# An attention and feed-forward kernel on one core: the steps of all five engines in one written list, in a new order, with PSUM as one tile of eight banks

## The chip, the cores and the metric

The kernel runs on one core of a Trainium2 chip. The core has five engines with an instruction queue each, which meet only through semaphores: TensorE (PE) for matmuls, ScalarE (ACT), VectorE (DVE), GpSimd (POOL), and SyncE (SP), which only starts DMAs. ACT and POOL can start DMAs too. Operands lie in SBUF; matmuls write to PSUM, which has eight banks of 512 f32 values per partition. The metric is the device time of one execution, in microseconds (us); lower is better.

## What is computed

Eight batches of attention with eight heads of width 64 over 576 positions, a causal window of 128 and a linear bias; then a feed-forward layer on its output, with a gated activation.

```python
B, H, S, D = q.shape                       # 8, 8, 576, 64
scores = (q @ k^T) / sqrt(D)
mask = (rel >= 0) & (rel < 128)            # rel = query position - key position
scores = where(mask, scores - slopes[h] * |rel|, -1e9)
attn = softmax(scores)
x = (attn @ v).transpose(0, 2, 1, 3).reshape(4608, 512)
h = x @ w_in                               # 512 -> 2048
g = h * (1.0 / (1.0 + exp(-beta * h)))
out = g @ w_out                            # 2048 -> 512, f32
```

Inputs and outputs are f32; the kernel multiplies in bf16 and accumulates in f32.

## The kernel before

**Attention.** q, k and v are loaded in f32 into staging tiles (`fst`, 14 buffers) and cast to bf16. For batches 0 and 1, full rows are handled by pairs of heads p = 0..3: q and k are cast into `bst` and transposed on PE (`TP`), and the result is copied to `QK`, for q by ACT and for k by DVE. For batches 2 to 7, and only there, blocks of 128 rows (sb = 0..4, the last of 64) are cast and then transposed by a DMA from SP (`DT`). The rows 512 to 575 of batches 0 and 1 have their own small steps (`TT`, `SCT`, `PV`, `X`).
Scores of K=64 go to two neighbouring banks of PSUM (`SP_` with the visits A and B for batches 0 and 1, `SC` for the others). ACT takes their exponential into `pt`, and DVE multiplies by a table of the bias and the mask (`factor`), unless a matmul has put the bias in beforehand ("biased"). Then `PVP` or `PVB` multiplies by v, with a column of ones for the sum; DVE divides (`norm`); and the result is transposed to `XT`, on PE (`XP`, `X`) for batches 0 to 3, by DMAs from SP for 4 to 7.

**Feed-forward.** The 4608 rows are cut into nine groups g of 512. Block `H(g, j)`, j = 0..15, is four matmuls 128x512 into one bank (`hps`, `hpo`, `SX`); ACT takes the tanh of half of beta*h (L564), and DVE forms (tanh + 1) * h into `gT` (L565). Output block (g, i), i = 0..3, is sixteen matmuls 128x512 in four parts `O(g, i, n)` (L588); then an eviction with the factor 0.5 into `osb` (L598, on ACT), and a store (L606). The last output block, (8, 3), is in two halves of 256 columns, in one bank; its second half is evicted by DVE (L596).

**What sets the order.** The first part, up to four H matmuls of j = 0 and 1, is written out by hand for all five engines, under `manual_schedule`. From there PE, SP and POOL follow the order in which the program's text issues steps, while ACT and DVE are ordered by the framework's scheduler. The text mixes steps by rules: `blocks(2)` with batch 2's loads, `jobs(b)` for later batches' loads, casts and transposes, `att` for attention steps with weights, and `spread` to deal them out between the H and O parts. PSUM comes from pools (`psum_c`, `psum_h`, `psum_t`, `psum_x`, later `psum_o`, `psum_s`), which decide the bank of each tile; a pool that is closed makes room for another.
All loads of q and k, and the first batches' v, are started by SP (L207, L218), all casts of loaded data are done by POOL (L228 to L243), which also starts the loads of the weights, W1 and W2 in four pieces each (L257, L261), and those of later v's (L250). Stores are started by POOL (g < 3), ACT and SP. Two gates hold steps back: the first DMA transpose of batch 2 waits for the last piece of W2, and `falls_late`, which fills a table, for the tanh of (1, 4).
A step in this text holds the matmuls and what ACT and DVE do with them. Idle matmuls on zeros (`idle`, `calm`) keep PE's clock up: 16 in all.

Of the kernel before, what the change touches and what calls it, by code (L numbers as in the profile page):

```python
# [15 lines left out]
P = 128  # L16


@with_exitstack
def kernel(  # L20
# [10 lines left out]
    nc = tc.nc  # L31
# [52 lines left out]
    psum_c = ctx.enter_context(tc.tile_pool(name="psum_c", bufs=1, space=bass.MemoryType.PSUM))  # L84
    psum_h = ctx.enter_context(tc.tile_pool(name="psum_h", bufs=2, space=bass.MemoryType.PSUM))
    trans = ExitStack()
    psum_t = trans.enter_context(tc.tile_pool(side="right", name="psum_t", bufs=2, space=bass.MemoryType.PSUM))
    SS = psum_c.tile([P, 2, 512], F32, name="SS")
    psum_c.seal()
    opening = ExitStack()  # L90
    psum_x = opening.enter_context(tc.tile_pool(name="psum_x", bufs=1, space=bass.MemoryType.PSUM))
    SX = psum_x.tile([P, 2, 512], F32, name="SX")
    late, gates = {"tick": 0}, {}
    spans = [SS]

    def span():

        spans.append(spans.pop(0))
        return spans[-1]

    def obank(name, tag=None):
        if tag is None:
            late["n"] = late.get("n", 0) + 1
            tag = "ops" if late["n"] % 2 else "h3"
        return late["o"].tile([P, DM], F32, name=name, tag=tag)[:]

    def after(ins, other):
        tc.add_manual_dep(
            ins.ins, other.ins.name,
            mybir.DependencyInfo(mybir.DependencyClass.Sync, mybir.DependencyReason.DATA),  # L110
            reason="gate",
        )

    def idle(n):
        for _ in range(n):
            nc.tensor.matmul(
                SS[:, 0, :], lhsT=zeros[:, 0:P], rhs=zeros[:], start=True, stop=True,
                skip_group_check=True)  # L120

    def constants():
# [4 lines left out]
        idle(8)  # L127
# [35 lines left out]
    def falls_late(i):  # L163
        to, a, w = ((0, 0, P), (128, 0, 64), (192, 0, P), (320, 1, 64), (384, 1, P))[i]
        after(nc.vector.tensor_copy(
            out=falls[:, :, to : to + w], in_=fall[:, :, a, 0:w]), gates[1, 4])

    def factor(pt, m, p):

        if m:  # L170
            nc.vector.tensor_tensor(  # L171
                out=pt[:], in0=pt[:], in1=falls[:, 2 * p : 2 * p + 2], op=ALU.mult)
            return
# [16 lines left out]
    def betas():  # L190
        bps = psum_t.tile([P, NFF], F32, name="bps", tag="t")
        nc.tensor.transpose(out=bps[:], in_=bflat[:], identity=identf[:])
        nc.vector.tensor_scalar_mul(beta_h[:], bps[:], 0.5)
# [7 lines left out]
    def get(what, b, sb):  # L201

        rows = ROWS[sb]
        src = {"q": q, "k": k, "v": v}[what]
        f = fst_pool.tile([P, H, D], F32, name="fst", tag="fst")
        fs[what, b, sb] = f
        return nc.sync.dma_start(  # L207
            out=f[0:rows],
            in_=src[b, :, P * sb : P * sb + rows, :].rearrange("h p d -> p h d"),
        )  # L210

    def get_pair(b, p):

        r = []
        for what, src in (("k", k), ("q", q)):
            f = fst_pool.tile([P, 2, 4, D], F32, name="fst", tag="fst")
            fs[what, b, "p", p] = f
            r.append(nc.sync.dma_start(  # L218
                out=f[:].rearrange("r h c d -> r h (c d)"),
                in_=src[b, 2 * p : 2 * p + 2, 0:FULL, :].rearrange("h (r c) d -> r h (c d)", c=4),  # L220
            ))
        return r[0]

    def cast_qk(b, sb):
        rows = ROWS[sb]
        t = bst_pool.tile([P, 2, H, D], BF16, name="bst", tag="bst")
        staged[b, sb] = t
        nc.gpsimd.tensor_copy(out=t[0:rows, 0], in_=fs.pop(("q", b, sb))[0:rows])  # L228
        return nc.gpsimd.tensor_copy(out=t[0:rows, 1], in_=fs.pop(("k", b, sb))[0:rows])  # L229

    def cast_pair(b, p):
        t = bst_pool.tile([P, 2, 4, 2 * D], BF16, name="bst", tag="bst")
        staged[b, "p", p] = t
        for i, what in ((1, "k"), (0, "q")):
            r = nc.gpsimd.tensor_copy(
                out=t[:, i].rearrange("r c (h d) -> r h c d", d=D),
                in_=fs.pop((what, b, "p", p))[:])
        return r

    def cast_v(b, sb):  # L240
        moved.add(("v", b, sb))
        rows = ROWS[sb]
        return nc.gpsimd.tensor_copy(  # L243
            out=VS[b % 2][0:rows, sb, :, 0:D], in_=fs.pop(("v", b, sb))[0:rows])
# [22 lines left out]
    pts, xns = {}, {}  # L267

    def calm(n):

        z = psum_h.tile([P, 512], F32, name="z", tag="hps")
        for _ in range(n):
            nc.tensor.matmul(
                z[:], lhsT=zeros[:, 0:P], rhs=zeros[:], start=True, stop=True,
                skip_group_check=True)

    def TP(b, p):
        src = staged.pop((b, "p", p))
        for i in (1, 0):
            if (b, p) == (0, 1):  # L280
                calm(1 + i)
            tps = psum_t.tile([P, FULL], BF16, name="tps", tag="t")
            to = tps[:].rearrange("d (c r) -> d c r", c=4)
            if i == 0:
                to = tps[:].rearrange("d (k c r) -> d c k r", k=4, c=4)
            for c in range(4):
                nc.tensor.transpose(out=to[:, c], in_=src[:, i, c], identity=ident[:])
            if i:
                nc.vector.tensor_copy(
                    out=QK[b % 2][:, 1, p, 0:FULL].rearrange("d (r c) -> d r c", c=4),  # L290
                    in_=tps[:].rearrange("d (c r) -> d r c", c=4))
            else:
                nc.scalar.copy(out=QK[b % 2][:, 0, p, 0:FULL], in_=tps[:])

    def TT(b):

        src = staged.pop((b, 4))
        tps = psum_t.tile([P, 2, NP, 64], BF16, name="tpt", tag="t")
# [7 lines left out]
        nc.scalar.copy(out=QK[b % 2][:, :, :, FULL:S], in_=tps[:])  # L306
# [6 lines left out]
    def SP_(b, vis, p):  # L313
        qk = QK[b % 2]
        sps = SX if vis == "B" else SS
        w = WIDTH[vis]
        biased = vis == "A" or p > 1
# [22 lines left out]
        pt = pt_pool.tile([P, 2, 512], BF16, name="pt", tag="pt")  # L340
        pts[b, vis, p] = pt
        nc.scalar.activation(out=pt[:, :, 0:w], in_=sps[:, :, 0:w], func=ACTF.Exp, scale=qscale)
        if vis == "B" and b and not biased:
            factor(pt, None, p)

    def room(b, shape):

        if b == 0:
            return psum_h.tile(shape, F32, name="pvh", tag="hps")[:]
        if "o" in late:  # L350
            return obank("pvo")[:, 0 : 4 * 66].rearrange("p (h x) -> p h x", x=66)
        return psum_t.tile(shape, F32, name="pv", tag="t")[:]
# [9 lines left out]
    def PVP(b, vis, p):  # L362
        vs = VS[b % 2]
        if vis == "A":
# [3 lines left out]
        pv = room(b, [P, 4, 66])  # L368
# [10 lines left out]
        norm(xn[:, q0 : q0 + 2, :].rearrange("p n (e d) -> p (n e) d", e=2), pv, P)  # L379

    def XP(b, p):
# [513 lines left out]
```

The softmax here doesn't subtract the row's maximum and nothing guards it: scores larger than these inputs give would overflow.

## Time and profile before

| | us |
|---|---|
| Time, median of three runs (range) | 325.57 (325.54 to 325.97) |
| Span of the profiled execution | 324.0 |
| PE busy | 312.7 |
| ACT busy | 194.1 |
| DVE busy | 183.1 |
| POOL busy | 98.8 |

The span is that of one profiled execution, from its first to its last instruction; the times of the runs lie about 1.57 above it, with what is around the span. Busy time is the sum of an engine's instructions; those that only start DMAs, branch or handle semaphores are not in it. PE's ends are modelled, so that its busy time is no measure of useful work, but a pause between matmuls is real. "SPq" and "ACTq" are the queues in which SP and ACT start DMAs. The first matmul starts at 1.19 us, and the last instructions are the eviction and the store of (8, 3).

### The profile page before, as it was taken

The numbers are of one execution on the slowest core, as the hardware profiler recorded it, in microseconds if no ns is written. First come the engines' busy times: TensorE is split into PE (matmuls) and PEld (weight loads), VectorE is DVE, ScalarE is ACT, GpSimd is POOL, SyncE is SP. The second block draws the span as 40 slices with busy tenths as digits, with TensorE's granted clock in tenths as the row PEclk, the third lists the DMA queues.
The fourth block names the chain that finished last, engine by engine and source line by source line (L and its number), as shares of the span: only waits on it lengthen the run. The fifth ranks groups of instructions, "written<-read, shape, count | busy, mean of one in ns | idle before, by whom it ended". The sixth has DMA issues, their size and how long they took to land.

```text
span 324.0 us, 5988 instructions
## 1 busy us (share of the span) xinstructions
PE 312.7 (97%) x2297; PEld 153.3 (47%) x2297; DVE 183.1 (57%) x346; ACT 194.1 (60%) x283; POOL 98.8 (30%) x154
## 2 busy tenths in 40 slices
PE   8888999999999999999999999999999999999995
PEld 3454554443545454544454545444544455444443
DVE  5777877542548753785178717752775176335500
ACT  6857887635558865685467635845675465346511
POOL 4864820333873455356226232340000000000000
PEclk9999999999999999999999999999999999999999
DMA  7999999998999999999969994993222112110021
GB/s 221 252 263 238 176 196 196 215 199 162 214 181 208 222 208 139 230 217 148 257 153 196 150 245 94 211 138 107 18 65 60 65 18 65 46 62 32 10 90 65
DMA packets 147565, 48.84 MB, mean 151 GB/s; under 512 B 135360, under 2 KB 143824, under 8 KB 147536
## 3 DMA queue, kind: packets, MB, share of 16 engines
q1 hardware_dynamic: 115712, 32.39, 56.1%
q0 software_dynamic: 28624, 10.29, 26.1%
q10 hardware_dynamic: 3200, 5.78, 5.1%
q8 instruction: 18, 0.29, 0.4%
q14 instruction: 11, 0.09, 0.1%
HBM read 36.71 MB, written 9.44 MB: 142 GB/s over the span
## 4 chain that ended last, share of the span: by engine, by line
PE 69%; DMA 17%; SPq 6%; POOL 2%; ACT 2%; DVE 2%; issue 1%; POOLq 0%; DVEq 0%
PE ops L588 21%; PE hps L557 21%; PE hpo L557 10%; PE oph L588 7%; DMA fst<-in_v_dram 6%; DMA qkT<-bst 6%; SPq L207 3%; DMA fst<-in_q_dram 3%; DMA fst<-in_k_dram 2%; PE SS L438 2%; SPq L218 2%; PE ST L438 1%; PE SS L495 1%; PE SS L492 1%; POOL bst L229 1%
## 5 line engine op out<-in xcount | busy, mean ns | idle before, releaser
L588 PE MATMUL ops<-W,gT 128*128 128x512 bf16 (+1 forms) x464 | 109.7, 372 | 0.5 <-ACT osb L598 0.5
L565 DVE SCALAR_TENSOR_TENSOR gT<-sig,hps 128x512 bf16<-128x512 bf16 x100 | 67.6, 683 | 71.8 <-ACT sig L564 71.5
L557 PE MATMUL hps<-XT,W 128*128 128x512 bf16 x400 | 99.9, 379 | 0.3 <-DVE XT L533 0.3
L564 ACT ACTIVATE sig<-hps,beta_h 128x512 bf16<-128x512 f32 x100 | 68.1, 690 | 34.6 <-PE hps L557 33.2
L588 PEld LDWEIGHTS <-gT 128*128 128x128 bf16 x592 | 55.7, 98 | 61.6 <-issue 1.9
L557 PEld LDWEIGHTS <-W 128*128 128x128 bf16 x576 | 52.9, 98 | 60.8 <-issue 3.6
L228 POOL CAST bst<-fst 128x512 bf16<-128x512 f32 (+1 forms) x32 | 20.8, 650 | 74.4 <-DMA fst<-in_q_dram 42.4
L557 PE MATMUL hpo<-XT,W 128*128 128x512 bf16 x168 | 43.1, 379 | 0.0
L564 ACT ACTIVATE sig<-hpo,beta_h 128x512 bf16<-128x512 f32 x42 | 29.0, 690 | 16.9 <-PE hpo L557 16.9
L565 DVE SCALAR_TENSOR_TENSOR gT<-sig,hpo 128x512 bf16<-128x512 bf16 x42 | 28.6, 681 | 11.2 <-ACT sig L564 11.0
L598 ACT ACTIVATE osb<-ops 128x512 f32<-128x512 f32 (+1 forms) x28 | 16.6, 595 | 25.5 <-PE ops L588 25.5
L446 ACT ACTIVATE pt<-SS 128x1024 bf16<-128x1024 f32 x24 | 24.5, 1020 | 11.6 <-PE SS L438 11.1
L588 PE MATMUL oph<-W,gT 128*128 128x512 bf16 x128 | 29.3, 379 | 0.0
L229 POOL CAST bst<-fst 128x512 bf16<-128x512 f32 (+1 forms) x32 | 22.1, 690 | 15.6 <-DMA fst<-in_k_dram 15.0
L176 DVE TENSOR_TENSOR pt<-pt,fall 128x1024 bf16<-128x1024 bf16 x24 | 17.1, 712 | 14.8 <-ACT pt L446 14.8
L446 ACT ACTIVATE pt<-ST 128x1024 bf16<-128x1024 f32 x24 | 24.5, 1022 | 0.0
L171 DVE TENSOR_TENSOR pt<-pt,falls 128x1024 bf16<-128x1024 bf16 x24 | 18.8, 791 | 9.3 <-ACT pt L446 9.3
L250 POOL DMA_DIRECT2D vs<-in_v_dram x25 | 21.3, 869 | 0.2 <-issue 0.2
L598 ACT ACTIVATE osb<-oph 128x512 f32<-128x512 f32 x8 | 4.8, 597 | 21.1 <-PE oph L588 21.1
L495 PEld LDWEIGHTS <-pt 128*128 128x128 bf16 x240 | 14.8, 97 | 4.2
L243 POOL CAST vs<-fst 128x512 bf16<-128x512 f32 (+1 forms) x15 | 10.5, 703 | 15.9 <-DMA fst<-in_v_dram 15.9
L438 PEld LDWEIGHTS <-qkT 64*128 64x128 bf16 x240 | 8.9, 94 | 12.5 <-issue 12.0
(102 smaller groups left out, 257.8 us busy)
## 6 DMA issues: line engine op xcount, KB each, us to landing
fst<-in_k_dram SPq DMA_DIRECT2D x32, 256.0 KB, 6.0
fst<-in_q_dram SPq DMA_DIRECT2D x32, 256.0 KB, 5.3
out_dram<-osb ACTq DMA_DIRECT2D x22, 256.0 KB, 2.0
fst<-in_v_dram SPq DMA_DIRECT2D x12, 256.0 KB, 5.4
out_dram<-osb POOLq DMA_DIRECT2D x12, 256.0 KB, 5.2
vs<-in_v_dram POOLq DMA_DIRECT2D x20, 128.0 KB, 6.1
W<-in_moe_w_in_dram POOLq DMA_DIRECT2D x4, 512.0 KB, 7.9
W<-in_moe_w_out_dram POOLq DMA_DIRECT2D x4, 512.0 KB, 12.8
```

The lines of the kernel that those rows point to most:

```text
L171: nc.vector.tensor_tensor(out=pt[:], in0=pt[:], in1=falls[:, 2 * p : 2 * p + 2], op=ALU.mult)
L228: nc.gpsimd.tensor_copy(out=t[0:rows, 0], in_=fs.pop(("q", b, sb))[0:rows])
L229: return nc.gpsimd.tensor_copy(out=t[0:rows, 1], in_=fs.pop(("k", b, sb))[0:rows])
L250: return nc.gpsimd.dma_start(out=VS[b % 2][0:rows, sb, :, 0:D], in_=v[b, :, P * sb : P * sb + rows, :].rearrange("h p d -> p h d"))
L438: nc.tensor.matmul(o, lhsT=qk[64 * e : 64 * e + 64, 1, p, P * kb : P * kb + P], rhs=qk[64 * e : 64 * e + 64, 0, p, P * kb : P * kb + nq], ...
L446: nc.scalar.activation(out=pt[:], in_=sps[:], func=ACTF.Exp, scale=qscale)
L495: nc.tensor.matmul(o, lhsT=weights(b, qb, h, 0), rhs=vs[:, qb, h, 0 : D + 1], start=qb == 0, stop=True, skip_group_check=True)
L557: nc.tensor.matmul(hps, lhsT=W1[:, c, bass.ts(j, P)], rhs=XT[:, c, c0 : c0 + TOKG], start=(c == 0), stop=(c == NDM - 1),)
L564: gates[g, j] = nc.scalar.activation(out=sig[:], in_=hps, func=ACTF.Tanh, scale=beta_h[:, j : j + 1])
L565: gates["gT"] = nc.vector.scalar_tensor_tensor(out=gts[g][:, j, :], in0=sig[:], scalar=1.0, in1=hps, op0=ALU.add, op1=ALU.mult)
L588: nc.tensor.matmul(ops_[:, cols], lhsT=gT[:, j, i * P : i * P + P], rhs=W2[:, j, cols], start=(j == 0), stop=(j == NFF - 1),)
L598: nc.scalar.mul(o, ops_[:, cols], 0.5)
```

## The change

A text `PLAN` of steps replaces both the part written by hand and the rules. Each step is `name.engine:arguments`, the engine being p for POOL, v for DVE, a for ACT, s for SP; a loop reads the list and issues every step, under `manual_schedule` for all five engines. What was one step is now several, with a place each: `H` (matmuls), `a` (tanh) and `d` (DVE's product); `S`, `E` (exp) and `M` (factor); `V` and `n` (norm); `X` and `x` (copy); `O`, `oc` (eviction) and `st` (store); `Rk`/`Rq` (transpose) and `rk`/`rq` (copy); `k`, `q`, `gk`, `gq`, `gv` (loads) and `ck`, `cq`, `cK`, `cQ`, `cv` (casts). The last number of a matmul step is its bank (before the flag of `A` and `B`, which says whether the bias is put in by a matmul; before the columns' range in `h`).

The number of matmuls and their kinds are the same, 2297 with the 16 idle ones; their order is new from the start. Among the other engines:

- Loads on these two queues: 37 of 95 are started by ACT, the others by SP (all by SP before).
- Casts of loaded data: 41 on POOL, 32 on DVE, 22 on ACT (95 on POOL before).
- Output evictions: 16 on ACT, 21 on DVE; stores: 17 from POOL, 10 from ACT, 10 from SP.
- The copies after PE's transposes go to ACT or DVE step by step.
- Both gates are gone. The halves of (8, 3) (`OL`) have a bank each.

```diff
+PLAN = """
+q.s:0:0 k.a:0:0 q.s:0:3 gv.s:0:1 k.s:0:1 q.s:0:1 k.s:0:2 q.a:0:2 k.s:0:3 const cq.p:0:0 ck.v:0:0
+z:1:5 z:2:0 cq.v:0:3 Rk:0:0:4 fr:5 fr:4 order ck.v:0:1 cq.v:0:1 cq.v:0:2 Rq:0:0:3 rk.a:0:0 rq.a:0:0
+gv.s:0:2 gv.s:0:0 A:0:0:6:1 EA:0:0 ck.p:0:2 Rk:0:1:3 B:0:0:0:0 gv.s:0:3 z:2:2 Rq:0:1:7 Rq:0:3:6
+k.s:1:1 q.s:1:1 q.s:1:0 Rq:0:2:4 Rk:0:2:5 ck.v:0:3 cv.p:0:2 EB:0:0 fr:2 rq.a:0:3 rq.a:0:2 rq.v:0:1
+rk.v:0:1 w1:0 rk.a:0:2 Rk:0:3:0 A:0:2:1:1 cv.p:0:0 ones cv.v:0:1 rk.a:0:3 EA:0:2 MB:0:0 A:0:1:6:1
+z:1:4 fr:7 EA:0:1 B:0:1:1:0 B:0:3:4:1 EB:0:1 VA:0:0:6 VA:0:1:3 nA:0:0 B:0:2:6:1 cv.a:0:3 VB:0:0:0
+nA:0:1 EB:0:3 EB:0:2 MB:0:1 fr:3 k.s:1:0 VB:0:3:1 A:0:3:2:1 w1:1 nB:0:3 nB:0:0 k.s:1:2 VB:0:1:5
+cq.a:1:0 EA:0:3 beta:4 VB:0:2:4 w1:2 gv.s:1:1 VA:0:3:6 nB:0:1 XP:0:0:3 VA:0:2:1 XP:0:1:0 q.s:1:2
+ck.a:1:0 nB:0:2 xc.a:0:0 cq.p:1:1 z:2:5 q.s:1:3 Rq:1:1:5 Rk:1:0:7 gq.s:0:4 cq.p:1:2 xc.a:0:1
+gv.s:1:0 nA:0:3 XP:0:3:6 ck.a:1:1 nA:0:2 XP:0:2:3 xc.a:0:2 Rq:1:0:4 rq.a:1:1 w1:3 rk.a:1:0 xc.v:0:3
+rq.v:1:0 Rk:1:1:1 k.a:1:3 H:0:3:2 h:0:0:0:0:3 rk.v:1:1 gv.s:1:3 gk.s:0:4 a:0:3 h:0:0:0:3:4 fr:1
...
+MCT:1 d:1:0 d:1:7 d:1:13 cK.p:2:3 O:0:0:3:2 O:0:1:1:3 D:2:1
+PV:1:0:4 d:1:2 nV:1:0 d:1:14 PV:1:1:6 O:0:2:2:7 O:0:2:3:7 oc.a:0:0 S:2:0:0:1 S:2:0:3:4 nV:1:1 D:2:4
...
+E:2:1:2 x.a:1:4 O:1:0:1:5 O:0:3:2:3 E:2:1:3 O:1:1:2:2 M:2:0:2 O:1:1:3:2 O:0:3:3:3 gv.s:2:4 st.p:0:2
+M:2:1:2 M:2:0:0 M:2:1:3 oc.v:0:3 cv.v:2:4 O:1:0:2:5 V:2:0:6 O:1:2:0:0 oc.a:1:1 n:2:0 O:1:2:1:0
...
+O:8:0:3:3 O:7:0:3:2 oc.v:8:1 oc.v:7:0 oc.a:8:2 OL:1:1 lc.v:1 st.p:8:1 oc.a:8:0 OL:0:2 ls.a:1 lc.a:0
+ls.a:0 st.p:8:2 st.s:8:0 st.p:7:0
+"""
...
-    psum_c = ctx.enter_context(tc.tile_pool(name="psum_c", bufs=1, space=bass.MemoryType.PSUM))
-    psum_h = ctx.enter_context(tc.tile_pool(name="psum_h", bufs=2, space=bass.MemoryType.PSUM))
-    trans = ExitStack()
-    psum_t = trans.enter_context(tc.tile_pool(side="right", name="psum_t", bufs=2, space=bass.MemoryType.PSUM))
-    SS = psum_c.tile([P, 2, 512], F32, name="SS")
...
+    psum = ctx.enter_context(tc.tile_pool(name="psum", bufs=1, space=bass.MemoryType.PSUM))
+    PS = psum.tile([P, 8, 512], F32, name="PS")
+    psum.seal()
+
+    def bank(k):
+        return PS[:, k, :]
...
+    def move(eng, out, in_):
+        (nc.scalar.copy if eng is nc.scalar else eng.tensor_copy)(out=out, in_=in_)
...
+    def cast_pair(what, eng, b, p):
+        if (b, "p", p) not in staged:
+            staged[b, "p", p] = bst_pool.tile([P, 2, 4, 2 * D], BF16, name="bst", tag="bst")
+        move(eng, staged[b, "p", p][:, "qk".index(what)].rearrange("r c (h d) -> r h c d", d=D),
+             fs.pop((what, b, "p", p))[:])
...
-        if (b, sb) == (2, 0):
-            after(r, w2[3])
...
+    with tc.manual_schedule(engines={ENG.PE, ENG.SP, ENG.Pool, ENG.Activation, ENG.DVE}):
+        for step in PLAN.split():
+            name, *at = step.split(":")
+            name, _, eng = name.partition(".")
+            STEPS[name](*([ENGINES[eng]] if eng else []), *map(int, at))
```

`STEPS` maps each name to its function. `const` stands for `constants()`: there the load of beta (`bflat`) is started by ACT, followed on ACT by the load of its function table, a warming activation and eight exponentials (`fallq`). `fr` fills rows of a table, `w1` and `w2` load a piece of the weights.

## The prediction

> **What bounds the kernel now.** I read the page's totals first, then the busy time by stretch, then TensorE's waits, then ACT's opening.
>
> ```profile
> span 324.0 us, 5988 instructions
> PE 312.7 (97%) x2297; PEld 153.3 (47%) x2297; DVE 183.1 (57%) x346; ACT 194.1 (60%) x283; POOL 98.8 (30%) x154
> PEclk9999999999999999999999999999999999999999
> PE 69%; DMA 17%; SPq 6%; POOL 2%; ACT 2%; DVE 2%; issue 1%; POOLq 0%; DVEq 0%
> ```
>
> PE is busy 97% at full clock; ACT and DVE are under 61%. The change keeps all 2297 matmuls, so only PE's idle time can be won. Where is it? Columns: stretch, length, busy time and count of PE, PEld, DVE, ACT, POOL, then clock, DMA share, GB/s.
>
> ```profile
> 0.00:10.00 10.00, 7.93 (x48) 3.60 (x49) 6.72 (x28) 7.12 (x15) 5.19 (x16) 1.00 0.84 233
> 10.00:20.00 10.00, 8.90 (x124) 5.03 (x124) 7.04 (x21) 7.21 (x11) 8.81 (x15) 1.00 1.19 272
> 20.00:30.00 10.00, 9.32 (x65) 4.30 (x64) 7.74 (x15) 7.37 (x13) 3.34 (x5) 1.00 1.09 229
> 30.00:40.00 10.00, 9.19 (x99) 4.68 (x100) 7.83 (x18) 7.87 (x12) 8.84 (x15) 1.00 1.02 188
> 40.00:50.00 10.00, 9.12 (x113) 5.26 (x109) 7.12 (x18) 7.85 (x13) 2.01 (x4) 1.00 1.23 196
> 50.00:100.00 50.00, 48.96 (x352) 23.25 (x350) 26.11 (x47) 29.74 (x42) 22.54 (x34) 1.00 1.21 193
> 200.00:250.00 50.00, 50.00 (x358) 24.20 (x357) 31.98 (x56) 31.65 (x45) 6.59 (x9) 1.00 0.67 101
> ```
>
> PE's idle time is 5.5 us in the first 50 (2.07 + 1.10 + 0.68 + 0.81 + 0.88), 1.0 in 50 to 100, 0.8 in 100 to 200 (by the same view), nothing to 300, and 3.9 at the end: 0.64 between starts at 317.9, and 3.3 of tail. About 11 us in all; 200 to 316 can't improve. PE's longer waits:
>
> ```profile
> PE tps L287 <- POOL bst L235: 1.8, 4, 0.7
> PE SS L438 <- DMA qkT<-bst: 1.3, 3, 0.5
> PE SS L118 <- DVE warm L125: 1.2, 1, 1.2
> PE ops L588 <- ACT osb L598: 0.5, 1, 0.5
> ```
>
> PE waits in the opening for POOL's casts, later for a few DMA transposes, and at the end for ACT to read the bank that the last half shares. ACT's start, in order of time (start, length):
>
> ```profile
> 0.74 0.44 ACTq L124 DMA_DIRECT2D bflat<-in_moe_beta_dram  x1
> 1.21 1.28 ACT L126 ACT_TABLE_LOAD   x1 [1.21 <-PEq L879]
> 2.61 2.54 ACT L142 ACTIVATE fallq<-relq 128x256 bf16<-128x256 f32 x8
> 6.00 0.59 ACT L293 COPY qkT<-tps 128x512 bf16<-128x512 bf16 x1 [0.84 <-PE tps L287]
> ```
>
> **What the skill says.** The Trainium skill, "TensorE: Matmul & The Clock Gate" (What's actually happening), has a matmul of 512 columns at some 216 ns warm and half the clock until about 3.4 us of sustained work. The trace agrees: 0.216 us between starts, but 0.427 for the eight zero matmuls before 4.7 us. "DMA: Bandwidth & Descriptors" (Issuing engines are not separate DMA queues) says that issuing from several engines saves only the sequencer's time. Here an SP load takes 0.44 to 0.6 us to issue, but 1.1 to 2.2 where loads are outstanding, so moving loads buys no bandwidth. "VectorE: DVE Perf Modes" (TRN2 errata, its table) prices an SBUF copy at twofold rate at (58 + 512/2)/0.96, 0.33 us; no row of before is a 512-wide f32 cast from SBUF on DVE.
>
> **The change, part by part.**
>
> *PE order and banks.* Nothing is added or removed on PE. Stretches where K=64 scores meet other matmuls cost some 0.1 us at each switch; by the instruction order there are 94 such switches before and 88 after: −0.6, of which I take −0.5. One PSUM tile could have meant waits on the whole tile; in the built program 218 of the 235 waits of PE for ACT or DVE readers are for readers of the same bank, so that is worth nothing. A bank's next use stands typically 2 us of PE work after the last, but under 0.5 in 26 of 77 uses in the first 30 us: there a late ACT or DVE is a PE stall at once.
>
> *The end.* The halves of (8,3) get banks 1 and 2: the gap at 317.9, 0.64 between starts where 0.11 is usual, goes: −0.5. The tail (3.3 us: last eviction, issue, landing) keeps its form: 0. What covers the other late stores is three or more us of matmuls.
>
> *Casts off POOL.* 54 of 95 casts leave POOL: 32 to DVE, 22 to ACT. POOL's spacing is 0.557 us, so −30 us there, in the opening on the path (1.8 above). DVE pays 32 × 0.33 = +10.7 (bounds 0.33 by the skill's price and 0.61, the spacing of its PSUM copies, which would be +19.5). ACT pays 22 × 0.52 = +11.4 (bounds 0.47, its PSUM copies, and 0.61). Both have over 120 us idle, so by sum this costs nothing. By order it can: these queues are in order, and a cast waits for its load. Before, only POOL stood at such waits. `ck.a:1:0`, `cq.a:1:0` on ACT and `cv.v:2:0`, `cv.v:2:4` on DVE stand at most 5 us of PE work behind their loads in the list, and loads land 2.8 to 6 us after issue, 14 to 19 beside weights. Behind the DVE ones wait factors and `d` steps, on which PE's banks hang. SP may issue ahead of the list, which shortens this. I take +0.5 for all after the opening (0 to +3).
>
> *Evictions and stores.* Of the output evictions 16 of 37 stay on ACT (36 before); 21 are on DVE at 0.6 each where ACT paid 0.484 between starts. `qkT` and XT copies are split between ACT and DVE. With the casts this brings ACT's work from about 184 to 202 us (issues at 0.58 counted in) and DVE's from 164 to 189, of 324: free by sum. POOL issues 17 stores instead of 12 (0.56 each), in an engine that lost 30 us: 0.
>
> *Loads on ACT, and the semaphores of DMAs.* 37 loads leave SP (−17 us of issue); with 8 + 2 stores against 22, ACT's DMAs go from 23 to 48. In the trace such an issue runs under the preceding ACTIVATE (205.58 to 205.94, inside a tanh that began at 205.42), so 25 more cost next to nothing when nothing is waited for; uncovered, 25 × 0.45 = 11 us on ACT. But in the built order each DMA of SP or ACT waits until the one eight before it on a shared list has landed; before, only SP's did. The first: `bflat`, behind `k.a:0:0`. In the trace the first k load landed at 3.55; on two queues I put it at 4.2. ACT then does 0.44 + 1.28 + 0.20 + 2.54: its first copy at 8.7 instead of 6.0, +2.7.
>
> *The opening as a sum.* ACT gets in addition two more copies from PSUM (2 × 0.48) and three casts (3 × 0.52), +2.5, so +5.2 against the 5.4 us that it idled between 6.0 and 22.3 (0.43, 0.39, 0.61, 0.24, 0.43, 0.34, 1.10, 1.84). Not all of that idleness can be used, because half of it follows PE's products. I put the first hidden block `H:0:3` at 22.7; PE of before had done as much (12.4 us of matmuls) at 21.5: +1.2. PE's pause near 6.6 to 9.6 is just short of the time that would cool the clock. From 21.5 to 49 before has gaps of 0.55, 0.82, 0.32, 0.13, 0.27, 0.65, 0.45, 3.2 in all; with batch 1's casts on three engines and transposes spread among the H blocks two thirds go: −2.2.
>
> *The rest.* Of 1.8 us idle in 50 to 200, mainly `qkT` transposes (0.44 and 0.71 at 74 and 96) and bank waits, two thirds go, since SP is relieved and D's sit 5 to 20 us behind their casts: −1.2. The removed gate on D:2:0 and on the falls copies frees them, hidden under H(1): 0 (if it met the W2 loads, the nearest row is the longest wait for a transpose above, 0.5).
>
> Sum: +1.2 − 2.2 − 1.2 − 0.5 − 0.5 + 0.5 = −2.7; span 324.0 → 321.3. The median shown, 325.57, is 1.57 over the profiled span; so **322.9**.
>
> **Rivals.**
> A, *nearly all gaps go*: ACT's late start disappears in its idle time (0), 21.5 to 49 wins 3.2, 50 to 200 wins 1.8, switches 0.6, end 0.5: −6.1, 319.5. For it: both engines have room. Against: 26 tight bank uses in the opening, and a floor of 2.7 more on ACT.
> B, *slower: ACT is held at a cast in the opening.* `ck.a:1:0` stands ahead of all three XT copies on ACT and waits for `k.s:1:0`, the sixteenth load. Before, the sixteenth landed at 22.5, with W1 pieces issued at 10.5, 15.2, 18.3; in the new POOL order pieces 0 to 2 follow `cv.p:0:2` and `cv.p:0:0` at once, near 12 to 14, and take bandwidth from it. Landing at 22.5 gives 22.5 + 0.5 + three copies and a cast, 2.0: `H:0:3` at 25.2, +3.7. Only 0.5 is recovered by 49, since ACT stays full; with +2.0 of cast and DMA waits in the middle (within my 0 to 3), −0.7 won there, −0.5 and −0.5: +3.5, 329.1. It decides where that landing passes about 21 us. Against: SP has fewer loads and reaches this one earlier.
> C, *no change*: 200 to 316 is full, and the opening's loss (+2.5) meets −2.5 elsewhere: 325.6.
>
> **How the numbers follow.** Main case 0.38 (319.9 to 324.9: opening 0 to +3 and stalls 0 to +2 around the sum), A 0.18, B 0.34, C 0.10. Faster or slower by 0.2% (0.65 us, about what this measurement can tell from no change): the main case and A are faster but for a little, 0.55; C mostly within, 0.09; B and the rest slower, 0.36. Range 318.0 to 329.7: down past A, up to B with some of its stalls; each end leaves about one in ten. The forecast's own range is the main case's.
>
> **What would show it.** Right: ACT's table load after 4.5 us and first qkT copy near 8.7; no wait before the last half; idle in 20 to 50 near 1 us instead of 2.4; SP's long issues gone. Wrong: ACT waiting for a load's landing in front of the XT copies with PE idle behind (B); PE below full clock near 8 us; DVE standing at `fst` with PE's `hps`/`S` banks waiting; H(1) beginning later than 49.

## The result, and the profile after

The changed kernel takes 330.53 us (median of four runs, 329.31 to 330.90) against 325.77 us in the same comparison (325.54 to 326.02): a ratio of 1.0147, 95% interval 1.0125 to 1.0169. It is slower by 1.5%. The forecast was 322.9, with a range up to 329.7.

The comparisons leave out runs more than 1.5% above the fastest of their kernel; several variants below spread more widely than that, so their lowest and highest times are given beside the median.

The page of the changed kernel, to be read against the same lines of before:

```profile
span 327.5 us, 5948 instructions
PE 310.0 (95%) x2257; PEld 155.0 (47%) x2297; DVE 202.8 (62%) x401; ACT 190.0 (58%) x282; POOL 65.0 (20%) x105
PEclk9799999979999999999999999999999999999999
PE 84%; DMA 6%; ACT 4%; DVE 2%; issue 1%; ACTq 1%; SPq 1%; POOL 0%; POOLq 0%; DVEq 0%
```

The span is 3.5 us longer. (Forty matmul records are missing; all 2297 weight loads are there.) The work moved as intended: POOL 98.8 to 65.0 us, DVE up by 20. The chain names DMA and POOL less than before. But twice the clock of PE drops, in the second and the ninth slice. The stretches:

```profile
0.00:10.00 10.00, 6.09 (x25) 2.74 (x25) 5.32 (x25) 4.88 (x12) 2.16 (x11) 1.00 0.88 251
10.00:20.00 10.00, 8.63 (x100) 4.90 (x97) 5.59 (x16) 8.24 (x12) 4.74 (x7) 0.83 1.21 258
20.00:30.00 10.00, 9.56 (x105) 5.99 (x105) 8.23 (x22) 9.47 (x17) 0.89 (x2) 1.00 1.19 228
40.00:50.00 10.00, 9.89 (x128) 6.01 (x129) 8.45 (x25) 7.56 (x12) 3.44 (x7) 1.00 1.19 204
50.00:100.00 50.00, 46.08 (x331) 22.43 (x335) 29.96 (x57) 27.87 (x41) 10.07 (x16) 0.97 1.11 191
150.00:200.00 50.00, 47.68 (x347) 23.17 (x351) 34.34 (x64) 27.74 (x38) 10.65 (x15) 1.00 1.20 167
```

From 20 to 50 us PE is fuller than before (9.56 where it was 9.32, 9.89 where it was 9.12). The first ten have 6.09 for 7.93; 50 to 100 has 46.08 for 48.96, some of it at a lower clock; 150 to 200 has 47.68 for 49.48. PE's longer waits, over the whole run:

```profile
PE PS L633 <- ACT pc L486: 3.5, 1, 3.5
PE PS L422 <- ACT qkT L206: 3.2, 2, 2.7
PE PS L633 <- DMA XT<-xn: 2.0, 1, 2.0
PE PS L411 <- DVE xnp L439: 0.6, 1, 0.6
```

Three long stops (3.5, 2.7 and 2.0 us), and none was there before. The wait for `osb` at the end is gone. The one at 64.5 us was the dearest, and ACT's row of work shows it in order of time:

```profile
61.06 0.69 ACT L641 ACTIVATE sig<-PS,beta_h 128x512 bf16<-128x512 f32 x1 [0.18 <-PE PS L633]
61.20 0.60 ACTq L307 DMA_DIRECT2D fst<-in_v_dram  x1
66.26 0.62 ACT L206 CAST bst<-fst 64x512 bf16<-64x512 f32 x1 [4.51 <-DMA qkT<-bst]
66.33 0.37 ACTq L307 DMA_DIRECT2D fst<-in_k_dram  x1
66.79 0.68 ACT L641 ACTIVATE sig<-PS,beta_h 128x512 bf16<-128x512 f32 x1
67.37 1.00 ACT L486 ACTIVATE pc<-PS 128x1024 bf16<-128x1024 f32 x1
```

The cast is `cQ.a:2:4`. Its data was there. It waits to write: staging tiles `bst` have four buffers, and the one that it gets was that of (2, 0), which the DMA transpose D:2:0 was still reading. That transpose was issued at 54.84 and landed at 66.24, 11.4 us later, beside two pieces of W2 (issued 54.02 and 54.75, landed 61.26 and 65.58). ACT works its queue in order: a tanh and the exponential of `SCT:1`, for whose banks PE was waiting, stood behind the cast. PE's starts are 3.88 us apart at 64.54, and the next seven matmuls come about 0.43 apart instead of 0.216, 1.5 us more.

To see where time goes when two kernels order their matmuls differently, I set each matmul of a trace against the matmul work issued before it (0.216 us for 512 columns, others in proportion, half for K=64, of which two run side by side; where a record is missing, the weight load stands for it), and compared the traces at equal work. Difference to the kernel before, in us, with the variants that come below:

| matmul work done | time before | changed | beta's load on SP | cast later | long rows | long rows, beta on SP |
|---|---|---|---|---|---|---|
| 6 | 12.4 | +3.1 | +0.1 | +3.6 | +3.2 | +0.1 |
| 12 | 21.1 | +3.2 | +0.2 | +3.6 | +3.2 | +0.2 |
| 24 | 36.6 | +0.5 | −2.4 | +1.3 | +0.6 | −2.4 |
| 33.7 (H(1) begins) | 49.0 | −0.7 | −0.6 | +0.1 | −0.6 | −2.9 |
| 48 | 63.9 | −0.7 | −0.6 | +0.1 | −0.6 | −1.9 |
| 54 | 70.2 | +4.1 | +3.2 | −0.2 | −0.9 | −2.2 |
| 75 | 93.2 | +3.2 | +2.2 | +2.0 | −1.9 | −3.2 |
| 110 | 131.2 | +2.4 | +1.9 | +1.3 | −3.4 | −4.7 |
| 190 | 214.7 | +4.0 | +3.9 | +2.9 | −4.0 | −5.3 |
| 290 | 316.1 | +4.0 | +3.9 | +2.9 | −4.0 | −5.3 |

Single rows can move by a us or two with the order of small pieces; the steps are what counts. At H(1) exactly the same matmuls are done in both kernels, so that row is exact. The opening lost 3.2, and by H(1) the changed kernel was 0.7 ahead (H(1) begins at 48.33 instead of 49.01). The stop at 64.5 cost 4.8. Some 0.8 was regained from 75 to 110, and 2.0 lost in one stop at 191.8.

### The profile page after: what moved, and what is told of

It is laid out like the page before. It is cut to its first block, busy times and chain, and to the rows that moved or that the text cites. A ratio compares the mean times of both kernels' runs of the same rounds, so it can differ in the third digit from the quotient of the medians.

```text
span 327.5 us, 5948 instructions
## 1 busy us (share of the span) xinstructions
PE 310.0 (95%) x2257; PEld 155.0 (47%) x2297; DVE 202.8 (62%) x401; ACT 190.0 (58%) x282; POOL 65.0 (20%) x105
## 4 chain that ended last, share of the span: by engine, by line
PE 84%; DMA 6%; ACT 4%; DVE 2%; issue 1%; ACTq 1%; SPq 1%; POOL 0%; POOLq 0%; DVEq 0%
PE PS L656 35%; PE PS L633 33%; PE PS L523 4%; DMA qkT<-bst 3%; PE PS L578 2%; PE PS L575 2%; DMA XT<-xn 2%; PE PS L422 1%; DMA fst<-in_k_dram 1%; PE PS L454 1%; PE PS L411 1%; PE PS L667 1%; PE PS L370 1%; ACT sig L641 1%; ACT qkT L206 1%
## 5 line engine op out<-in xcount | busy, mean ns | idle before, releaser
L633 PE MATMUL PS<-XT,W 128*128 128x512 bf16 x558 | 136.2, 381 | 6.7 <-ACT pc L486 3.5
L641 ACT ACTIVATE sig<-PS,beta_h 128x512 bf16<-128x512 f32 x144 | 95.6, 689 | 71.7 <-PE PS L633 62.7
L656 PE MATMUL PS<-W,gT 128*128 128x512 bf16 x540 | 132.2, 381 | 1.4 <-DVE gT L646 0.2
L646 DVE SCALAR_TENSOR_TENSOR gT<-sig,PS 128x512 bf16<-128x512 bf16 x144 | 94.5, 682 | 57.0 <-ACT sig L641 56.6
L532 ACT ACTIVATE pt<-PS 128x1024 bf16<-128x1024 f32 x48 | 46.9, 1023 | 16.2 <-PE PS L523 15.9
L206 POOL CAST bst<-fst 128x512 bf16<-128x512 f32 (+1 forms) x34 | 21.5, 644 | 138.0 <-DMA fst<-in_q_dram 36.8
L587 DVE TENSOR_TENSOR xn<-PS,zb 128x512 bf16<-128x512 f32 (+1 forms) x30 | 20.7, 690 | 1.0
L578 PE MATMUL PS<-vs,pt 128*128 128x65 bf16 x240 | 17.1, 193 | 0.0
L523 PE MATMUL PS<-qkT 64*128 64x256 bf16 (+2 forms) x240 | 15.3, 250 | 0.2 <-DVE gT L646 0.2
L432 ACT ACTIVATE pt<-PS 128x768 bf16<-128x768 f32 (+1 forms) x16 | 14.4, 923 | 1.6 <-PE PS L422 1.6
L575 PE MATMUL PS<-vs,pt 128*128 128x65 bf16 x192 | 14.6, 193 | 0.0
```

The source lines that it names most:

```text
L206: (nc.scalar.copy if eng is nc.scalar else eng.tensor_copy)(out=out, in_=in_)
L523: nc.tensor.matmul(o, lhsT=qk[64 * e : 64 * e + 64, 1, p, P * kb : P * kb + P], rhs=qk[64 * e : 64 * e + 64, 0, p, P * kb : P * kb + nq], ...
L532: nc.scalar.activation(out=pt[:], in_=held.pop(("S", b, m, p)), func=ACTF.Exp, scale=qscale)
L575: nc.tensor.matmul(o, lhsT=weights(b, qb - 1, h, 1), rhs=vs[:, qb - 1, h, 0 : D + 1], start=True, stop=False, skip_group_check=True)
L578: nc.tensor.matmul(o, lhsT=weights(b, qb, h, 0), rhs=vs[:, qb, h, 0 : D + 1], start=qb == 0, stop=True, skip_group_check=True)
L587: nc.vector.tensor_tensor(out=xn[0:nq].rearrange("p (g h) d -> p g h d", g=2), in0=pv[0:nq, :, :, 0:D], in1=zs[0:nq].broadcast_to([nq, 2, ...
```

## The experiments

First theory: a few steps that stand in order at something late (the cast of 2:4 on ACT, beta's load on ACT, the transposes XD:4:3, 4:2, 4:4 behind a load on SP) cost their stops, and can be moved one by one. Rival: they stand there because transfers come when they come, and whatever is moved, PE meets the transfers a little later.

**The cast on another engine.**

```diff
-... gv.a:1:4 cQ.a:2:4 gk.a:2:3 ...
+... gv.a:1:4 cQ.p:2:4 gk.a:2:3 ...
```

> The changed kernel with one cast, cQ:2:4, on POOL instead of ACT; all else as it was. Theory: this cast writes a staging buffer that the transpose D:2:0 still reads, so ACT stands 4.5 us in order behind a DMA that lands at 66.2, PE stops for 3.7 us at 64.5 and then runs at half clock for seven matmuls (1.5 us). Off ACT, all of that goes: about 325.6 to 326.5, no PE gap of over 1 us between 60 and 75. Rival: PE would run into the scores of batch 2, whose transposes are as late, and only 0 to 1.5 us are won (329 to 330.5), with the gap moved to the L523 matmuls.

Measured: 329.74 us, from 325.1 to 336.0 in twenty runs; the ratio of the ten kept is 1.0062 (1.0037 to 1.0087). The execution that was profiled (span 334.2) is the longest of the twenty, so it shows what can follow, not the usual case. In it PE doesn't stop at 64.5. Instead it waits 3.8 us at the scores of batch 2 for their transposes, up to 2.7 at 79.3, then 3.9 for a norm on DVE, which stood 5.2 us at another cast (`cv.v:2:4`) for its load; POOL stood 9.5 us at the moved cast. The stop was real, and both expectations hold in part: it was removed, and in the median of all twenty what followed gave back nearly all of it.

**The transpose's company moved.**

```diff
-... x.a:0:4 w2:2 w2:3 H:1:9:3 cv.p:2:1 ...
+... w2:2 w2:3 cQ.p:1:4 xc.a:1:2 ...
```

> The changed kernel with the last two pieces of W2 put ahead of the cast cQ.p:1:4 in the list, which delays them on POOL by 6.9 us; the cast of 2:4 stays on ACT. Theory: D:2:0 took 11.4 us because it ran beside those two pieces (issued 54.0 and 54.8, landed 61.3 and 65.6; the transpose landed at 66.2); with them issued near 47 it lands some 4.5 us after its issue, at about 59.5, the cast is not held, and the gain is that of the cast's own removal: 325.6 to 326.5. Rival: the pieces then slow the loads ahead of the transposes by as much and the wait stays, 329 to 331.

Measured: 330.52 us (329.6 to 333.4), ratio 1.0170 (1.0117 to 1.0224). The rival. The pieces were issued at 45.95 and 46.68; the loads between then took the loss, D:2:0 was issued at 59.31 instead of 54.84 and landed at 65.32 instead of 66.24. PE waited 3.0 instead of 3.5. So the collision with W2 isn't a cause of its own: the bytes have to come before this point in either order. Nor was the gate that the change removed at fault: in the kernel before the same transpose was issued only at 63.80 and landed at 68.33, later than now.

**The opening.**

```diff
-        nc.scalar.dma_start(out=bflat[:], in_=moe_beta.rearrange("(j p) -> j p", p=P))
+        nc.sync.dma_start(out=bflat[:], in_=moe_beta.rearrange("(j p) -> j p", p=P))
```

> The changed kernel with the load of beta started by SP instead of ACT, so that ACT's table load doesn't stand behind the landing of the first k load. Theory: ACT's first copy is at 6.0 instead of 8.8, PE's wait of 2.7 us at 7.2 shrinks to under 0.5 and PE keeps its clock; since the first 24 us lost 3.4 to 4.4 us but only 0.4 was left at 36 us of PE work, part of it passes through: -1.5 to -2.5 at the end, about 328 to 329. Rival A: the loss had been made up for anyway by the waiting of others, within 0.5 of 330.5. Rival B: SP is held at that DMA's own wait and later loads come late: slower than 330.5.

Measured: 327.66 us (326.0 to 329.5), ratio 1.0071 (1.0036 to 1.0106), about 0.75% better than the changed kernel. The stop at 7 us is gone, and at 24 us of work this variant is 2.9 ahead of the changed kernel. Then it is lost at H(1). PE's timeline at that place, and ACT's before it (start, length, idle before):

```profile
48.37 1.89 PE L633 MATMUL PS<-XT,W 128*128 128x512 bf16 x8 [2.30 <-ACT XT L206]
```

```profile
46.17 0.60 ACTq L307 DMA_DIRECT2D fst<-in_q_dram  x1
46.88 0.69 ACT L641 ACTIVATE sig<-PS,beta_h 128x512 bf16<-128x512 f32 x1 [3.17 <-POOL bst L206]
47.46 0.58 ACT L206 CAST XT<-PS 128x512 bf16<-128x512 f32 x1
47.93 0.39 ACT L206 COPY XT<-PS 128x256 bf16<-128x256 bf16 x1
```

ACT stood 3.2 us, in order, at issuing the load `gq.a:1:4`: it gets a staging buffer only when POOL has cast another load out of it, and that one had come late. Behind it stood a tanh and the copies to XT that PE needs, so H(1) begins at 48.37, as it does in the changed kernel (48.33), whatever the opening did. By the trace nothing was left of the gain there. The executions profiled took 329.15 here and 329.31 in the changed kernel, so these two traces differ by less than the medians do, which are 2.9 apart; where the median run gained I can't show.

**The transposes to XT.**

```diff
-... cQ.v:6:0 n:4:4 H:4:7:4 ...           ... O:4:0:0:4 XD:4:3 XD:4:2 gk.s:7:3 XD:4:4
+... cQ.v:6:0 n:4:4 XD:4:3 XD:4:2 XD:4:4 H:4:7:4 ...           ... O:4:0:0:4 gk.s:7:3
```

> The changed kernel with the three transposes XD:4:3, 4:2, 4:4 right behind the norm of 4:4 in the list instead of behind the load gq.s:6:3, where SP stood 4.1 us for the landing of another DMA. Theory: they are issued 2 to 5 us earlier, PE's stop of 2.0 us at 191.8 goes: about 328.5. Rival: waits for the semaphore eight DMAs back only move, or the next wait takes its place: within 0.7 of 330.5.

Measured: 330.18 us (329.1 to 331.7), ratio 1.0148 (1.0109 to 1.0187). PE's stop there is 1.1 us instead of 2.0, and nothing of it is seen in the total: within 0.7 of before the edit, as the rival had it. In the trace the three are issued from 186.18 to 188.75, not earlier than the 183.86 to 186.52 of the changed kernel (this execution is 2.4 longer): the place in the list was not all that held them. (In this profile the stop near 64.5 was 5.1 us: it varies between runs.)

**The cast later on the same engine**, so that no other engine is burdened.

```diff
-... gv.a:1:4 cQ.a:2:4 gk.a:2:3 ...       ... a:1:2 cv.a:1:4 gq.a:3:4 ...
+... gv.a:1:4 gk.a:2:3 ...                ... a:1:2 cQ.a:2:4 cv.a:1:4 gq.a:3:4 ...
```

> The changed kernel with the cast cQ.a:2:4 six ACT steps later, just ahead of cv.a:1:4; it stays on ACT, and its transpose D:2:4 is not due before. Theory: ACT then does the two tanhs and the exponential that PE's banks need at 61.8 instead of 66.3; PE's stop at 64.5 and the slow matmuls after it go, and nothing on POOL is moved as it was when the cast went there: 325.5 to 327. Rival: after that PE meets the transposes of batch 2, which land at 66 to 74 whatever ACT does, and gives 2 to 4 us back at the scores (L523): 328 to 330.

Measured: 332.25 us (328.2 to 335.0), ratio 1.0234 (1.0198 to 1.0270): not better, slower. The profiled execution (span 326.4, the shortest of the six) shows PE without any gap from 50 to 70 us, and then DVE at the next late load (its timeline; the cast is `cv.v:2:4`, with two norms queued behind it), and PE waiting for those norms (its list of waits):

```profile
91.17 0.42 DVE L206 CAST vs<-fst 64x512 bf16<-64x512 f32 x1 [3.17 <-DMA fst<-in_v_dram]
91.51 0.19 DVE L586 RECIPROCAL zb<-PS 128x8 f32<-128x8 f32 x1
91.74 0.69 DVE L587 TENSOR_TENSOR xn<-PS,zb 128x512 bf16<-128x512 f32 x1
```

```profile
PE PS L575 <- DVE xn L587: 2.8, 1, 2.8
```

In the changed kernel that cast runs at 91.17 too, but without a wait, because PE arrives there later. The load landed at 90.50 there and at 91.15 here: moving the cast of 2:4 didn't bring it sooner.

**Three moves together.** The cast later, beta's load on SP, the XD transposes early (the diffs above).

> The changed kernel with three moves: the cast of 2:4 later, beta's load on SP, the transposes XD:4:3, 4:2, 4:4 early. Theory of separate holds: 4.5 + 2 + 1 off 330.5, 323 to 324, faster than before. Rival, that up to 200 us the loads set the pace (16 queues busy 1.1 to 1.3 of the time by the stretches, and H(1) beginning at 49.0 to 49.5 in all runs so far whatever the opening did): the gains before 49 us do not add, 325 to 326.5.

Measured: 330.93 us (328.4 to 333.1), ratio 1.0174 (1.0135 to 1.0214). The sum of separate holds, 323 to 324, fails; so do the 325 to 326.5 of its rival. In the profile (span 330.6) the same cast on DVE costs 3.4, and casts of q and k on POOL and DVE in the first 40 us another 3.6 (2.2 and 1.4).

**The division of casts and of loads, each undone as a whole.** All 95 casts on POOL:

```diff
-... ck.v:0:0 ... cq.v:0:3 ... cv.a:0:3 ... cQ.v:2:0 ...     (54 steps)
+... ck.p:0:0 ... cq.p:0:3 ... cv.p:0:3 ... cQ.p:2:0 ...
```

> The changed kernel with all 95 casts back on POOL, in the same places of the list; loads as changed. Theory: casts hold an engine in order when their load or their buffer is late; on POOL that holds no tanh and no exponential, so ACT's stop near 62 goes, but POOL hands the later casts on late (as in the run with one cast moved), so that transposes come late: 326.5 to 330. If dividing the casts were right and only one place wrong, it would be slower than the changed kernel: over 331. If dividing them is the whole cost: 325 to 326.

Measured: 345.01 us (343.8 to 349.6), ratio 1.0595 (1.0568 to 1.0621). All loads on SP:

```diff
-... k.a:0:0 ... q.a:0:2 ... gv.a:1:4 ... gk.a:2:3 ...       (37 steps)
+... k.s:0:0 ... q.s:0:2 ... gv.s:1:4 ... gk.s:2:3 ...
```

> The changed kernel with all loads started by SP, in the same places of the list; casts as changed. Theory: the loads on ACT cost by their first wait alone (beta behind k), so the gain is that of beta's load on SP, 327 to 328.5, and the stop at 64.5 stays. Rival A: SP issues later loads late, because it is held at waits of transposes that stand ahead of them: slower, 331 to 335. Rival B: ACT is freed at 60 to 68 too: 325 to 326.5.

Measured: 341.57 us (336.4 to 344.0), ratio 1.0407 (1.0351 to 1.0464). Both are far slower, by 14 and 11 us (the second by more than any expectation): in this order, dividing casts and loads is needed, and isn't what made the change a loss. In the profiles, with the casts on POOL (span 347.8, the longest of four) PE waits 5.4 for one in the opening and 7.8 for transposes of q and k; with the loads on SP 6.5 for those and 6.1 at the old place.

By now the theory of single holds had failed. A count from the traces pointed to what they share: loads of q, k and v landed by a given time.

| by | before | changed | cast later | three moves | casts on POOL | loads on SP |
|---|---|---|---|---|---|---|
| 50 us | 30 | 32 | 32 | 32 | 31 | 31 |
| 90 us | 53 | 52 | 52 | 52 | 51 | 52 |
| 110 us | 65 | 65 | 65 | 63 | 62 | 63 |
| 200 us | 111 | 111 | 111 | 109 | 102 | 108 |

To about 100 us the loads arrive at one pace, whoever starts or casts them. And the changed order needs them sooner: the scores of batch 2 are all done by 63.9 us of matmul work where before they ended at 69.7, and the last of its PV by 79.0 where it was 82.5. That holds for batch 2, beside which the dearest stop lies; the scores of batches 3 and 4 end later than before (at about 98 and 130 us of matmul work, where it was 96 and 123). Second theory: this delivery sets the pace up to 200 us, and the changed order has less to spare against it. Rival: the in-order waits hold at any speed of delivery. To tell them apart, the delivery itself has to be changed.

**The same bytes in longer pieces.** From batch 2 on the loads of q, k and v (those that cast on the way too) read rows of w_out: 2 KB in one piece for each partition instead of eight pieces of 256 B. These kernels don't compute the reference's attention from batch 2 on; instructions, waits and bytes are the same.

```diff
-            in_=src[b, :, P * sb : P * sb + rows, :].rearrange("h p d -> p h d"),
+            in_=src[b, :, P * sb : P * sb + rows, :].rearrange("h p d -> p h d") if b < 2 else
+                moe_w_out[P * sb : P * sb + rows, :].rearrange("p (h d) -> p h d", d=D),
```

> The changed kernel, whose loads of q, k and v from batch 2 on read rows of w_out of the same size instead: one piece of 2 KB for each partition and load where there were eight of 256 B. The bytes, the instructions and the waits are the same; what is computed is not the reference. Theory: up to 200 us the delivery of these loads sets the pace (by 90 us 52 of them had landed in the kernel before and in all variants of the changed one, whoever issued them), and the changed order needs each with less to spare: with faster delivery the stop at 64.5 and those behind late loads go, 322 to 326. Rival: the in-order waits (eight DMAs back, buffers, casts) are what holds, at any speed of delivery: 328.5 to 331.

> The kernel before with the same exchange of sources from batch 2 on. Theory: its order waits little for loads (1.3 us of PE's waits name a transpose), so it gains only 0.5 to 2: 323.5 to 325. Rival, that delivery holds it as much as the changed kernel: 320 to 322.5.

Measured: the changed kernel takes 322.00 us with long rows (320.9 to 323.9), ratio 0.9905 (0.9871 to 0.9940), 8.5 less than without; the kernel before takes 325.81 with them (325.0 to 326.5), ratio 1.0004 (0.9988 to 1.0020), no change that can be told. So the short pieces of these loads cost the changed order 8.5 us and the old one nothing measurable, and with fast delivery the new order is the faster by 1%. The third section of the page, changed kernel first, then with long rows:

```profile
DMA packets 147245, 48.84 MB, mean 149 GB/s; under 512 B 135360, under 2 KB 143824, under 8 KB 147216
```

```profile
DMA packets 94829, 48.84 MB, mean 153 GB/s; under 512 B 75456, under 2 KB 83920, under 8 KB 94800
```

The bytes are equal, the packets fewer by 52,000. A load started between 50 and 100 us lands 3.57 us after its issue (median) where it took 4.97; in the kernel before it is 3.93 for 4.56. By 90 us 55 of the loads counted above have landed, with long rows, in both kernels. The stretch from 50 to 200 us, in the kernel before, the changed kernel, and the changed kernel with long rows:

```profile
50.00:200.00 150.00, 148.19 (x1099) 72.10 (x1097) 88.01 (x152) 94.44 (x134) 64.02 (x93) 1.00 1.24 192
```

```profile
50.00:200.00 150.00, 142.88 (x1044) 70.10 (x1061) 99.70 (x181) 90.70 (x129) 36.98 (x54) 0.99 1.20 182
```

```profile
50.00:200.00 150.00, 148.57 (x1098) 73.70 (x1118) 105.58 (x192) 94.94 (x136) 40.36 (x57) 1.00 1.00 183
```

The waits that PE's list names in that stretch sum up to 1.8 us, 6.2 and 0.5. The cast of 2:4 ran at 61.92 without a wait, because D:2:0 had landed at 60.72. That transpose took 7.0 us instead of 11.4, though the median of the transposes of q and k issued from 50 to 100 us didn't fall (5.8 for 5.1): how much came from the loads themselves and how much from a lighter traffic beside D:2:0 isn't separated here.

**The place or the piece?** The exchange changed the place that is read as well.

```diff
+                moe_w_out[P * sb : P * sb + rows, :].rearrange("m (c d) -> (m c) d", d=D).rearrange("(h p) d -> p h d", h=H),
```

> As the changed kernel with long rows: the loads from batch 2 on read w_out, but again in eight pieces of 256 B for each partition, in the pattern of q. The same place, the old piece. Theory, that the number of pieces sets the delivery: as the changed kernel, 329 to 332, with the stop near 64.5. Rival, that the place does (a small region read again and again): as with long rows, 321 to 323.

Measured: 330.57 us (327.5 to 331.6), ratio 1.0147 (1.0108 to 1.0185), the changed kernel's own. It is the length of the pieces, and with it their number, not the place.

**The opening with fast delivery.** Long rows, and beta's load on SP.

> The changed kernel with long rows from batch 2 on, and beta's load on SP. Theory: the opening's 3 us are regained at 20 us and given back before H(1), which waits for batch 1, whose loads are not changed: 321 to 322.3, PE waiting 2 us for XT near 46. Rival: with delivery fast, they pass through: 318.5 to 320.

Measured: 320.09 us (319.2 to 322.0), ratio 0.9823 (0.9782 to 0.9863). It lies between the two expectations: of the 3 us won in the opening, 2.3 are left at H(1) and 1.3 at the end. I had held that batch 1's loads, whose pieces are unchanged, would hold H(1). But what had held it, ACT at the issue of `gq.a:1:4`, is nearly gone: that comes at 43.88 us here instead of 46.17, ACT's idle time before the tanh behind it is 0.96 instead of 3.17, and the starts before H(1) are 0.46 apart. That fits buffers coming free sooner.

**One part alone on the kernel before**: the second half of (8, 3) in its own bank.

```diff
+            dst = obank("ol", "h3") if at else ops_
...
-                    ops_[:, cols], lhsT=gT[:, j, i * P : i * P + P], rhs=W2[:, j, cols],
+                    dst[:, cols], lhsT=gT[:, j, i * P : i * P + P], rhs=W2[:, j, cols],
...
```

The two evictions read `dst` as well.

> The kernel before with one part of the change alone: the second half of output block (8, 3) in a bank of its own. The prediction's step: 0.5 off, 324.8 to 325.1. Rival: the wait of 0.5 moves to the last eviction or store, within 0.2 of before.

Measured: 325.28 us (323.9 to 327.9), ratio 0.9990 (0.9967 to 1.0013). The wait of 0.5 us is gone from the trace; whether the time follows can't be told at this spread.

**A version with the real data that beats both?** Two last tries at moving holds. The four moves are the three above, and `cv.v:2:4` behind `x.v:2:2`; the two are beta's load and the XD transposes.

```diff
-... oc.v:0:3 cv.v:2:4 O:1:0:2:5 ...      ... x.v:2:2 E:3:0:0 ...
+... oc.v:0:3 O:1:0:2:5 ...               ... x.v:2:2 cv.v:2:4 E:3:0:0 ...
```

> The changed kernel with four moves: the three of the run before of that kind (the cast of 2:4 later on ACT, beta's load on SP, XD:4:3, 4:2, 4:4 early), and the cast cv.v:2:4 later on DVE, behind the copy x.v:2:2, two norms and two evictions after its old place, since DVE stood there for 3.2 to 5.2 us when the first hold was gone. Theory, that each removed hold brings the next while the loads come when they come: 327 to 331. Rival, that these four were the holds: 322 to 325, faster than before.

> The changed kernel with two moves: beta's load on SP and the transposes XD:4:3, 4:2, 4:4 early; the casts where they are. Theory: as with beta's load alone, less up to 1: 326.5 to 328. Rival, that the two add in full: 325 to 326.

Measured: 328.17 us (327.7 to 329.6), ratio 1.0091 (1.0058 to 1.0125), and 328.71 (327.1 to 331.8), ratio 1.0092 (1.0059 to 1.0125). With four holds gone the trace is 2.4 us ahead of before at 75 us of work and 2.0 behind at 110. The waits of PE from 36 us on, four moves:

```profile
PE PS L523 <- DMA qkT<-bst: 2.6, 1, 2.6
PE PS L633 <- ACT XT L206: 2.1, 1, 2.1
PE PS L633 <- DMA XT<-xn: 1.2, 1, 1.2
```

Now PE itself waits for a transpose of q and k. Each removed hold brought the next, as the second theory says. No version with the real data beat the kernel before.

## Why the prediction was wrong

The side was wrong: slower, where the forecast was faster. The time lies 0.8 us above the range, and the profiled span 6.2 above the predicted 321.3. Nearly all of it comes after H(1) begins: up to there the prediction's terms give −1.0 and the traces −0.7, from there to the end −1.7 and +4.2. By its steps:

- *The casts by order* are the step that failed: "+0.5 for all after the opening (0 to +3)". PE's listed waits from 50 to 200 us are 6.2 us where they were 1.8. One cast alone cost about 5 (3.5 of wait and 1.5 of half clock), and the stop at 191.8 another 2.0. What the runs showed in place of this step: the new order meets loads that have not arrived, and with their pieces lengthened 8.5 us go, nearly all of these waits among them. I had counted the distance of each cast from its load, and let SP run ahead of the list. I had not counted that a cast also waits for the staging tile's last reader, four tiles back, a DMA. And I had asked how far each wait was in the list, never how many loads would have landed by then: 53 by 90 us in the profile of before was there to be counted. The prices were right: casts on DVE stand 0.33 us apart (96.78 and 97.11), as the Trainium skill's table ("VectorE: DVE Perf Modes", TRN2 errata) gave in the prediction, and one on ACT 0.51 from the next instruction (20.36 to 20.87), where I had 0.52.
- *The rest*, −1.2 in 50 to 200, had the same fault. Two thirds of the 1.8 us of waits were to go; with the real loads late transfers put 6.2 in their place, and only with long rows, at 0.5, did the two thirds go.
- *Loads on ACT, and the semaphores of DMAs*: for the first case, on ACT, the mechanism and the size were right. The later cases had no term, and one was dear: at the load `gq.s:6:3` SP stood 4.1 us for an earlier load of k to land, with the XD transposes of the stop at 191.8 behind it. Beta's load was issued at 4.54 after the first k load had landed, and the first copy came at 8.77 (8.7 predicted). ACT's start in the profile:

```profile
4.54 0.35 ACTq L216 DMA_DIRECT2D bflat<-in_moe_beta_dram  x1
4.92 1.28 ACT L218 ACT_TABLE_LOAD   x1 [4.92 <-DMA fst<-in_k_dram]
6.32 2.54 ACT L234 ACTIVATE fallq<-relq 128x256 bf16<-128x256 f32 x8
8.77 1.04 ACT L206 COPY qkT<-PS 128x512 bf16<-128x512 bf16 x2
```

- *The opening*: `H:0:3` was put at 22.7 us and began at 24.35, so against the 21.5 of before the loss was 2.9 instead of 1.2. Beta's load alone accounts for it: started by SP, it leaves `H:0:3` at 21.36. That ACT's idle time couldn't take up the late start because half of it follows PE is my reading; the clock did drop, to 0.83 in 10 to 20 us, which I had thought just avoided. But from there to H(1) 3.5 came back, where 2.2 was predicted (PE's idle time in 20 to 50 us is 0.6). That the sum of both came out at −0.7 for −1.0 is luck: the two misses cancel.
- *The removed gate*, 0 with 0.5 at most: the transposes did meet W2, and D:2:0 took 11.4 us instead of 4.5; yet it landed earlier than before the change. The gate was rightly priced; the cast that wrote the tile next was not.
- *The end*, −0.5, is there in the trace; alone on the kernel before it is below what the runs can tell. *The switches*, −0.5, weren't tried alone.
- *Rival B* had the time (329.1) and the kind of cause, ACT held in order at a cast, but at the wrong place: `ck.a:1:0` ran at 21.57 without a wait for its load. That its time came out is luck in part: its +3.7 in the opening was taken from that landing (and 22.5 + 0.5 + 2.0 is 25.0, not its 25.2), and its middle term, +2.0, was too small. The Trainium skill's sentence that starting DMAs from several engines saves only the sequencer's time ("DMA: Bandwidth & Descriptors", Issuing engines are not separate DMA queues) agrees with the counts of landed loads up to 90 us (52, whether ACT starts some of them or none), and it should have led me to ask whether the new order needs the loads sooner. It is not all that counts here: with all loads on SP the kernel takes 11 us longer, and its trace has SP standing at transposes and stores, with loads queued behind them.

## What to carry to other kernels

Before costing a new order by its waits, set when it needs each transfer against how many have landed by then in the old trace: an order with PE 97% busy can be one that just fits the delivery, and a tighter one hits it. A cast or copy on a compute engine waits for its load and for the last reader of its buffer, and everything behind it in order waits too; but moving it only pays where the transfer itself isn't late. To find out which, keep bytes and instructions and change only the pieces of the transfers.

## What the runs showed of the hardware that was not expected

The length of the pieces alone was worth 8.5 us of 330 in this order: a load, mostly 256 KB, took 4.97 us to land (median) in 1024 pieces of 256 B, and 3.57 in 128 pieces of 2 KB. The Trainium skill, "DMA: Bandwidth & Descriptors" (Why small descriptors are slow (HBM only)), gives a fixed cost for each packet, 27% at 256 B, by its count of cycles; the times here are 39% apart, with other transfers and queues in them, so they agree in kind only.

PE fell to half its clock after pauses shorter than I had counted on. "TensorE: Matmul & The Clock Gate" (What's actually happening) has it after an idle window of some 3.4 us. Starts 3.88 us apart at 64.54 were followed by a granted clock of 0.50, which fits. But in the opening starts 3.04 us apart were too: the clock was 0.50 from 10.00 to 13.42, after 3.41 us in which PE worked 0.69. Nor does the length of the pause alone decide: with beta's load on SP, starts 2.67 us apart at 64.58 were followed by 0.50 from 68.16 to 71.57, while with all loads on SP starts 3.84 us apart at 117.28 were followed by matmuls at full spacing, 0.22.

Times also spread differently: 325.1 to 336.0 in twenty runs of the first variant, against 324.1 to 330.1 in 25 of the kernel before. What makes them spread isn't shown.
